# Batch 6 takes its gate logits with the gate weights as stationary operand, and the order's model gives the last batch's logits another duration

## The chip, the cores and the metric

The kernel runs on one core of one Trainium2 chip. The metric is the device time of one execution, in microseconds (us). The core's engines are named as in the profile: PE is TensorE's matmul, PEld its load of the stationary operand, DVE is VectorE, ACT is ScalarE, POOL is GpSimd, SP is SyncE.

## What is computed

Windowed attention (four heads with a plain window of 32 keys, four with a window of 32 keys that lie 4 apart) over 8 batches of 576 tokens gives 4608 rows of 512 values. Each row then goes to one of 8 experts, and the assignment is greedy over all pairs of token and expert:

```
x = attn(q, k, v)                     # (4608, 512), float32
logits = x @ w_gate                   # (4608, 8)
for idx in argsort(-logits.flatten()):        # best pair first
    tok, e = idx // 8, idx % 8
    if assigned[tok] < 0 and counts[e] < 576: # capacity of an expert
        assigned[tok] = e; counts[e] += 1
for e in range(8):
    out[assigned == e] = relu(x[assigned == e] @ w1[e]) @ w2[e]
```

## The kernel before, in words

There are two stages: `attention`, which also computes the logits, and `moe`, which searches the experts' thresholds (`R.alone` for the first), gathers the tokens, and runs two matmuls per expert. The first search needs the logits of all 4608 tokens, so the last logits of `attention` stand between the stages.

In `attention` the work is cut into 32 units, four for each batch b: unit u = 4b + 2 kind + ui, where kind 0 is the plain window and kind 1 the dilated one. On PE a unit runs a bfloat16 pass for the row maxima (L486), then three groups of scores (L503 for mask and maximum, L506 for the float32 product), then the product with the values in two groups (L514). ACT takes the exponential (L456), DVE divides by the sum (`weigh`, L520 and L526). For each batch, seven "turns" of three transposes each (L564) bring the rows into `xt` with the features on the partitions. A "keep" (L272 on ACT, L575 on DVE for the very last) copies each turn out of PSUM. The PSUM tiles of the values, the turns and the logits come from one pool of three (`PV`).

The logits have two forms.

- The weights stationary (`banks`, batches 0 to 5, L597 on): for each half of a batch, four matmuls, one per block of 128 features. The gate weights, padded to 32 columns, are the stationary operand and 288 tokens move. The four blocks land in four bands of 32 partitions. DVE copies the result to `L4` (L605), transposes on PE (`gates`, L616) turn it chunk by chunk of 128 tokens, and a DVE reduction (`settle`, L622) adds the four bands into `Lt`. All of `xt` of the batch must be there first.
- The tokens stationary (`tokens`, batches 6 and 7, L654): four steps, one per feature block. Each runs five matmuls (four chunks of 128 tokens and one of 64) with 8 columns moving. Steps 0 and 1 need the plain turns only, step 2 the turns of the first dilated unit, step 3 all of them. A copy on DVE (L664) and one on ACT (L272) bring the result into `Lt`. Each float32 matmul is recorded as two MATMULs, so a step shows as x10; a transpose is recorded as one.

A batch ends with `R.choose` (L869 to L879 on DVE: best expert and its key) and `coarse` (L755 on DVE, L760 on PE: counts against coarse thresholds). The counts of all chunks form one chain in order of the chunks. A batch of 576 tokens is 4.5 chunks, so an odd batch's first half chunk shares its column of `Lt` with the batch ahead. `DIRECT` is the first batch of the second form.

The order on each engine is written out by a planner (`Schedule.run`). Each step has a modelled cost, dependencies and a boost. `left` is the longest modelled path from a step to the end, with 180 added for each change of engine. `due` is the whole length minus `left` minus boost. A step with larger `left` plus boost is taken first. Where the first in line isn't ready, the planner fills in steps that end by the modelled start of the first plus a tolerance (800 on PE). The boost of unit u has -4680 u in it; values have 14500 more, the weights-stationary logits and batch 6's turns -5200, batch 7's turns and logits 3000.

Of the kernel before, what the change touches and what calls it, by code (L numbers as in the profile page):

```python
# [14 lines left out]
OP = mybir.AluOpType  # L15
AX = mybir.AxisListType
# [3 lines left out]
B, H, S, D = 8, 8, 576, 64  # L20
N = B * S
DM = H * D
NE, FF = 8, 1024
# [15 lines left out]
B_L, B_G, B_T, B_X, B_H, B_HL, B_Y, B_S, B_W = 23000, 27000, 15000, 0, 20000, 17000, 28000, -15000, 1500  # L39
RAW1, D_R, NQ, AHEAD_W = 8, 262, (2, 2), (3,)  # L40
ADDED, T_A, T_G = (("2", 0), ("1", 1), ("2", 1)), 4500, 4500
NS, B_E, DIRECT = (2, 2), 3000, 6
B_C = (0, 2500, 20000, 20000, 20000, 20000, 20000, 20000)
P_U, B_A, B_K, B_V, B_P, TOL_A, TOL_B, TOL_C, TOL_D = 4680, 15400, -5200, 14500, -105500, 650, 650, 300, 800
Q_ENG = (("POOL", "POOL", "POOL", "ACT"), ("DVE", "DVE", "ACT", "ACT"))
# [197 lines left out]
def attention(tc, ctx, C, load_const, T, xd, Lt, R):  # L243
    nc = tc.nc
# [5 lines left out]
    op = K.op  # L250

    def ring(pool, shape, dtype, name, n):
        return Ring([pool.tile(shape, dtype, name=f"{name}{i}") for i in range(n)])
# [13 lines left out]
    L4 = ring(pk, [128, 2 * S], F32, "L4", 1)  # L267
# [43 lines left out]
    ready = {}  # L311
# [69 lines left out]
    class Unit:  # L381
# [40 lines left out]
        def build(self):  # L422
# [56 lines left out]
            if ui == 1:  # L479
                for k, f in enumerate(stores(b, kind, xs)):  # L480
                    usex.append(op("SP", 475, f, Unit.xsd, -u * P_U - 5000, dma=128 * S * 4 * 2 / 4 / D_R))
            banks(self, xs, list(Unit.xsd), usex)

        def scan(self, c0, c1, pm):
# [58 lines left out]
    xt_ = {}  # L543

    def banks(un, xs, done, usex):

        b, kind, ui, u = un.b, un.kind, un.ui, un.u
        if ui == 0:
            if kind == 0:
                xt_[b] = []  # L550
            xt_[b, kind] = XT[kind].take()
        xt, oldt, uset = xt_[b, kind]
        for i in (() if kind == 0 and ui == 0 else range(3) if kind == 0 else (ui, 2 + ui)):
            pt = Buf(PV)

            def turn(i=i, pt=pt):
                t = pt.tile.rearrange("p (c x) -> p c x", c=4)
                for c in range(3):
                    if kind == 0:
                        src = xs[:, 3 * i + c].rearrange("p a d -> p (a d)")  # L560
                    else:
                        si, ch = divmod(i, 2)
                        src = xs[:, 3 * si + c, 2 * ch:2 * ch + 2].rearrange("p a d -> p (a d)")
                    nc.tensor.transpose(t[:, c], src, C["identf"])  # L564

            end = b == B - 1 and (kind, i) == (1, 3)

            def keep(i=i, pt=pt, act=nc.vector.tensor_copy if end else act):
                t = pt.tile[:, :384]
                if kind == 0:  # L570
                    act(xt[:, :, 192 * i:192 * i + 192].rearrange("p a (c i) -> p c a i", i=64),
                        t.rearrange("p (c a i) -> p c a i", c=3, a=2))
                else:
                    si, ch = divmod(i, 2)
                    act(xt[:, ch].rearrange("p (c i r) -> p r c i", c=3, r=DIL)[:, 2 * si:2 * si + 2],  # L575
                        t.rearrange("p (c a i) -> p a c i", c=3, a=2)[..., :48])

            late = B_K if b < B - 1 else B_E
            t = un.op("PE", 325, turn, done, late, pt)
            usex.append(t)  # L580
            k = un.op("DVE" if end else "ACT", 491 if kind == 0 else 620, keep, [t, *oldt], late)
            pt.users.append(k)
            xt_[b].append(k)
            if (kind, ui) == (1, 0):
                ch_.setdefault(b, []).append(k)
        if (kind, ui) != (1, 1):
            return
        if b >= DIRECT:
            return tokens(un)
        lg = L4_[b % 2] = []  # L590
        sm = []
        for j in range(2):
            pt = Buf(PV)

            def logits(j=j, pt=pt):
                for g in range(4):
                    nc.tensor.matmul(pt.tile[32 * g:32 * g + 32, :S // 2], wgp[:, g],  # L597
                                     xt_[b, g // 2][0][:, g % 2, 288 * j:288 * j + 288], start=True, stop=True)

            t = un.op("PE", 560, logits, [*xt_[b], ready["w"]], B_K, pt)  # L600
            for kk in range(2):
                xt_[b, kk][2].append(t)
            o = (b % 2) * S + 288 * j
            eng = "ACT" if b == B - 1 and j else "DVE"
            k = un.op(eng, 365, lambda o=o, pt=pt, eng=eng: (nc.vector.tensor_copy if eng == "DVE" else act)(  # L605
                L4.tiles[0][:, o:o + 288], pt.tile[:, :S // 2]), [t, *L4_["free"]], B_K)
            pt.users.append(k)
            lg.append(k)
            c0 = -(-b * S // 128) if j == 0 else sm[0][1]
            c0, c1 = (b * S // 128 if j == 0 else sm[0][1]), (b * S + 288 * (j + 1)) // 128  # L610
            pg = Buf(PV)

            def gates(c0=c0, c1=c1, pg=pg):
                for c in range(c0, c1):
                    o = (128 * c) % (2 * S)
                    nc.tensor.transpose(pg.tile[:, 128 * (c - c0):128 * (c - c0) + 128], L4.tiles[0][:, o:o + 128], C["identf"])  # L616

            t = un.op("PE", 107 * (c1 - c0), gates, [*L4_[0], *L4_[1]], B_K, pg)

            def settle(c0=c0, c1=c1, pg=pg):  # L620
                n = c1 - c0
                nc.vector.tensor_reduce(Lt[:, c0:c1], pg.tile[:, :128 * n].rearrange(  # L622
                    "p (c g e) -> p c e g", c=n, g=4)[:, :, :NE], axis=AX.X, op=OP.add)

            x = un.op("DVE", 60 + 35 * (c1 - c0), settle, [t], B_K)
            pg.users.append(x)
            sm.append((x, c1, t))
        L4_["free"] = [x[2] for x in sm] if b % 2 else []
        c0, c1 = b * S // 128, (b * S + S) // 128
        x = un.op("DVE", 800, lambda: R.choose(c0, c1), [x[0] for x in sm], B_K)  # L630
        coarse(c0, c1, x, B_P)

    def coarse(c0, c1, x, late):
        for c in range(c0, c1):
            g, used, use_ = PRE.take()
            f = op("DVE", 290, lambda c=c, g=g: R.coarse(c, g), [x, *used], late)
            counted[0] = op("PE", 60, lambda c=c, g=g: R.coarse_counts(c, g), [f, ready["c", 3], counted[0]], late)
            use_.append(counted[0])

    def tokens(un):  # L640

        b, u = un.b, un.u
        c0, c1 = b * S // 128, (b * S + S) // 128
        parts = [(c, 0, 128) for c in range(-(-b * S // 128), c1)]
        half = (c0, 64, 64) if b % 2 else (c1, 0, 64)
        late = B_K if b < B - 1 else B_E
        pt = Buf(PV)
        o = lambda c, p, n: pt.tile[p:p + n, NE * (c - c0):NE * (c - c0) + NE]

        def logits(gs):  # L650
            for c, p, n in parts + [half]:
                for g in gs:
                    t0 = 128 * c + p - b * S
                    nc.tensor.matmul(o(c, p, n), xt_[b, g // 2][0][:, g % 2, t0:t0 + n], wgp[:, g, :NE],  # L654
                                     start=(c == parts[0][0] and g == 0), stop=(g == 3), skip_group_check=True)

        t = un.op("PE", 550, lambda: logits([0]), [*xt_[b][:3], ready["w"]], late, pt)
        t = un.op("PE", 550, lambda: logits([1]), [t], late)
        t = un.op("PE", 550, lambda: logits([2]), [t, *ch_[b]], late)
        t = un.op("PE", 550, lambda: logits([3]), [t, *xt_[b]], late)  # L660
        for kk in range(2):
            xt_[b, kk][2].append(t)
        ca = parts[0][0]
        xs_ = [un.op("DVE", 200, lambda: nc.vector.tensor_copy(  # L664
            Lt[:, ca:c1], pt.tile[:, NE * (ca - c0):NE * (c1 - c0)].rearrange("p (c e) -> p c e", e=NE)), [t], late),
            un.op("ACT", 250, lambda: act(Lt[half[1]:half[1] + 64, half[0]], o(*half)), [t], late)]
        pt.users += xs_
        if b < B - 1:
            hl_.append(xs_[1])
        x = un.op("DVE", 1000, lambda: R.choose(c0, c1), [*xs_, *(hl_ if b == B - 1 else ())], late)  # L670
        coarse(c0, c1, x, B_P if b < B - 1 else late - u * P_U)

    ch_, hl_ = {}, []
# [40 lines left out]
    for u in range(4 * B):  # L714
        b = u // 4
# [754 lines left out]
```

## Time and profile before

| | |
|---|---|
| median of 3 runs | 720.18 us (719.60 to 720.63) |
| the profiled execution's own time | 720.37 us |
| its span, first to last instruction | 718.6 us |
| PE busy | 678.6 us, 94% of the span |
| DVE, ACT busy | 484.2 us, 291.1 us |
| granted TensorE clock, mean over the span | 0.961 of full speed |

The profile is of one execution, and times in it are counted from the span's start. "Granted clock" is the share of full speed that TensorE was given: 1.00 is 2.4 GHz and 0.50 is 1.2 GHz. `attention` takes about the first 211 us. Matmuls overlap in the pipeline, so in a list of them the step from one start to the next tells more than a duration.

### The profile page before, as it was taken

How to read it: one execution, taken by the hardware profiler on the slowest of the kernel's cores; microseconds unless marked ns; L12 is line 12 of the kernel's file. 1: busy time of each engine (PE TensorE's matmuls, PEld its weight loads, DVE VectorE, ACT ScalarE, POOL GpSimd, SP SyncE). 2: the span in 40 equal slices, each digit the busy share in tenths (PEclk: the TensorE clock that was granted, in tenths of full speed). 3: DMA queues.
4: the chain of work that ended last, by engine and by line, in shares of the span. 5: the costliest groups of instructions: out<-in, count | busy, mean ns of one | idle time of the engine just before them, and what ended most of it. 6: DMA issues, size and time to landing. Idle time of an engine off the chain costs nothing.

```text
span 718.6 us, 17416 instructions
## 1 busy us (share of the span) xinstructions
PE 678.6 (94%) x6598; PEld 596.5 (83%) x6598; DVE 484.2 (67%) x2081; ACT 291.1 (41%) x617; POOL 137.3 (19%) x204
## 2 busy tenths in 40 slices
PE   7899999999984799799999999999999999999995
PEld 5788889998973598589889879788978978988984
DVE  5578877698237689579679868868978963823300
ACT  3355454543310383575334423514533434423310
POOL 6111111100000332741410310311221031221011
PEclk9999999999975799999999999999999999999998
DMA  9999999972111674978223513511532383122001
GB/s 249 260 269 294 264 301 267 281 198 55 47 35 36 207 147 106 292 172 238 96 67 118 169 63 92 200 45 52 167 135 67 118 291 130 56 74 97 1 22 45
DMA packets 58525, 104.62 MB, mean 146 GB/s; under 512 B 6212, under 2 KB 27844, under 8 KB 58436
## 3 DMA queue, kind: packets, MB, share of 16 engines
q1 hardware_dynamic: 49096, 78.32, 38.0%
q0 software_dynamic: 9344, 25.17, 12.8%
q8 instruction: 52, 0.85, 0.5%
q14 instruction: 33, 0.27, 0.1%
HBM read 78.31 MB, written 18.87 MB: 135 GB/s over the span
## 4 chain that ended last, share of the span: by engine, by line
PE 74%; issue 11%; DVE 6%; DMA 4%; POOL 3%; ACT 1%; POOLq 0%; SPq 0%; DVEq 0%
PE ph L1290 24%; PE py L1332 15%; PE pS L506 9%; PE px L514 6%; PE px L564 3%; PE pS L503 3%; DMA xg<-xd,idx 2%; PE pm L486 2%; PE pz L768 2%; PE ptx L1253 2%; PE px L654 2%; PE py L1335 1%; PE py L1337 1%; POOL out L1358 1%; DMA qs<-in_qd 1%
## 5 line engine op out<-in xcount | busy, mean ns | idle before, releaser
L1332 PE MATMUL py<-w2h,hb 128*128 128x512 f32 x512 | 173.6, 403 | 1.4 <-ACT w2h L1127 1.3
L1290 PE MATMUL ph<-xh,w1h 128*128 128x256 f32 (+1 forms) x512 | 138.7, 301 | 0.0
L1290 PE MATMUL ph<-xl,w1h 128*128 128x256 f32 (+1 forms) x512 | 136.2, 297 | 0.0
L1290 PE MATMUL ph<-xh,w1l 128*128 128x256 f32 (+1 forms) x512 | 136.0, 296 | 0.0
L1332 PEld LDWEIGHTS py<-w2h,hb 128*128 128x128 f32 x512 | 97.3, 190 | 21.8 <-ACT w2h L1127 2.3
L1332 PE MATMUL py<-w2l,hb 128*128 128x512 f32 x256 | 101.3, 396 | 0.8 <-DVE w2l L1128 0.5
L1127 ACT ACTIVATE hb<-ph 128x256 fp32r<-128x256 f32 (+2 forms) x192 | 59.7, 346 | 103.1 <-PE ph L1290 102.3
L1290 PEld LDWEIGHTS ph<-xh,w1h 128*128 128x128 f32 x512 | 91.5, 190 | 0.4
L1290 PEld LDWEIGHTS ph<-xh,w1l 128*128 128x128 f32 x512 | 91.6, 190 | 0.0
L1290 PEld LDWEIGHTS ph<-xl,w1h 128*128 128x128 f32 x512 | 91.5, 190 | 0.0
L506 PE MATMUL pS<-q,k 128*80 128x96 f32 (+1 forms) x672 | 84.2, 267 | 0.0
L1358 POOL DMA_INDIRECT out<-y,idx x40 | 40.1, 1003 | 205.9 <-ACT y L1127 145.0
L456 ACT ACTIVATE E<-pS 96x384 f32<-96x384 f32 (+1 forms) x96 | 46.7, 486 | 71.5 <-PE pS L506 70.4
L1310 DVE SCALAR_TENSOR_TENSOR hb<-ph,hb 128x320 fp32r<-128x320 f32 (+1 forms) x128 | 57.4, 453 | 26.5 <-ACT hb L1127 22.5
L506 PEld LDWEIGHTS pS<-q,k 128*80 128x80 f32 (+1 forms) x672 | 69.7, 161 | 0.1
L1127 ACT ACTIVATE y<-py 128x512 f32<-128x512 f32 (+1 forms) x40 | 23.9, 596 | 104.9 <-PE py L1332 90.1
L493 DVE CUSTOM_DVE_ANT_0 junkm<-pm,const 128x80 bf16<-128x80 f32 (+1 forms) x336 | 59.4, 243 | 5.1 <-PE pm L486 4.5
L1332 PEld LDWEIGHTS py<-w2l,hb 128*128 128x128 f32 x256 | 48.8, 191 | 10.6 <-DVE w2l L1128 1.1
L514 PE MATMUL px<-v,E 81*64 81x65 f32 (+1 forms) x1344 | 47.7, 225 | 2.9 <-ACT E L456 2.4
L1127 ACT ACTIVATE w1h<-raw 128x512 fp32r<-128x512 f32 x64 | 38.5, 628 | 29.3 <-DVE oa L1060 22.0
L1239 POOL DMA_INDIRECT xg<-xd,idx x40 | 40.2, 1005 | 50.1 <-PE ph L1290 31.1
L1128 DVE TENSOR_TENSOR w2l<-raw,w2h 128x512 fp32r<-128x512 f32 x48 | 31.7, 685 | 26.4 <-ACT w2h L1127 22.9
(168 smaller groups left out, 1036.5 us busy)
## 6 DMA issues: line engine op xcount, KB each, us to landing
raw<-in_moe_w SPq DMA_DIRECT2D x128, 256.0 KB, 3.7
v<-in_vp SPq DMA_DIRECT2D x8, 780.0 KB
v<-in_vd SPq DMA_DIRECT2D x8, 650.0 KB
xd<-xs SPq DMA_DIRECT2D x16, 288.0 KB, 8.9
xd<-xs SPq DMA_DIRECT2D x32, 144.0 KB, 10.0
w2l<-raw POOLq DMA_DIRECT2D x16, 256.0 KB
qs<-in_qp SPq DMA_DIRECT2D x7, 576.0 KB, 8.6
k<-in_kp SPq DMA_DIRECT2D x7, 576.0 KB, 10.4
```

Of the source, the lines that this page charges most:

```text
L456: e = self.op("ACT", 380, lambda j=j, pS=pS: nc.scalar.activation(self.E[:self.nk, j * self.gs:j * self.gs + self.gs], pS.tile[:, :self.gs ...
L493: nc.vector.tensor_tensor_reduce(out=jk[:, c - c0, :nk], in0=pm[:, (c - c0) * nk:(c - c0 + 1) * nk], in1=mm[:, min(1, (c if self.kind == 0 ...
L503: nc.tensor.matmul(pS[:nk, c - c0], ls[:64 + n, c], self.r[:64 + n, :2 * nq], start=(c == c0), stop=False, skip_group_check=True)
L506: nc.tensor.matmul(pS[:nk, c - c0], self.Ks[c], self.Qm[c], start=False, stop=True, skip_group_check=True)
L514: nc.tensor.matmul(px[64 * a:64 * a + 64, c - c0], lh, self.V[c][a], start=True, stop=True)
L1127: act = lambda o, i, f=AF.Copy: nc.scalar.activation(o, i, f)
L1128: sub = lambda e, o, a, b: e.tensor_tensor(o, a, b, op=OP.subtract)
L1239: nc.gpsimd.indirect_dma_start(out=xg[:n], out_offset=None, in_=xd, in_offset=bass.IndirectOffsetOnAxis(ap=box[0][:n, m:m + 1], axis=0))
L1290: nc.tensor.matmul(o, a[:, d * 128:d * 128 + 128], b[:, d, c0:c1], start=((d, i) == pairs[0]), stop=((d, i) == pairs[-1]))
L1310: hl = op("DVE", 335 if j == 0 else 400, lambda: nc.vector.scalar_tensor_tensor(hb[:, CAP + c0:CAP + c1], o, 0.0, hb[:, c0:c1], op0=OP.max ...
L1332: nc.tensor.matmul(py, x, w, start=(f + i == 0), stop=(f == NF - 1 and i == 2))
L1358: s = nc.gpsimd.indirect_dma_start(out=out, out_offset=bass.IndirectOffsetOnAxis(ap=box[0][:n, m:m + 1], axis=0), in_=y[:n], in_offset=None)
```

## The change

`DIRECT` goes from 6 to 7: batch 6 takes its logits with the weights stationary, and only batch 7 with the tokens stationary. As batch 6 ends in half a chunk, its second half gets one transpose more (64 tokens, `over`) and one DVE reduction more, and batch 7's `choose` waits for that step in place of batch 6's copy on ACT. The modelled cost of each of batch 7's four steps goes from 550 to 1050. The extra transpose and reduction have no modelled cost.

```diff
-NS, B_E, DIRECT = (2, 2), 3000, 6
+NS, B_E, DIRECT = (2, 2), 3000, 7
...
-            def gates(c0=c0, c1=c1, pg=pg):
+            over = b == DIRECT - 1 and j == 1
+
+            def gates(c0=c0, c1=c1, pg=pg, over=over):
                 for c in range(c0, c1):
                     o = (128 * c) % (2 * S)
                     nc.tensor.transpose(pg.tile[:, 128 * (c - c0):128 * (c - c0) + 128], L4.tiles[0][:, o:o + 128], C["identf"])
+                if over:
+                    o = (128 * c1) % (2 * S)
+                    nc.tensor.transpose(pg.tile[:64, 128 * (c1 - c0):128 * (c1 - c0) + 128], L4.tiles[0][:, o:o + 64], C["identf"])
...
-            def settle(c0=c0, c1=c1, pg=pg):
+            def settle(c0=c0, c1=c1, pg=pg, over=over):
                 n = c1 - c0
+                if over:
+                    nc.vector.tensor_reduce(Lt[:64, c1], pg.tile[:64, 128 * n:128 * n + 128].rearrange(
+                        "p (g e) -> p e g", g=4)[:, :NE], axis=AX.X, op=OP.add)
...
+            if over:
+                hl_.append(x)
...
-        t = un.op("PE", 550, lambda: logits([0]), [*xt_[b][:3], ready["w"]], late, pt)
-        t = un.op("PE", 550, lambda: logits([1]), [t], late)
-        t = un.op("PE", 550, lambda: logits([2]), [t, *ch_[b]], late)
-        t = un.op("PE", 550, lambda: logits([3]), [t, *xt_[b]], late)
+        t = un.op("PE", 1050, lambda: logits([0]), [*xt_[b][:3], ready["w"]], late, pt)
+        t = un.op("PE", 1050, lambda: logits([1]), [t], late)
+        t = un.op("PE", 1050, lambda: logits([2]), [t, *ch_[b]], late)
+        t = un.op("PE", 1050, lambda: logits([3]), [t, *xt_[b]], late)
```

## Rows read from the trace of the kernel before

**Rows 1.** Stretches: us, then busy time (instructions) by engine, granted clock, DMA share, GB/s
```profile
170.00:180.00 10.00, 10.00 (x165) 9.52 (x162) 7.02 (x58) 4.80 (x10) 0.00 (x0) 1.00 0.21 51
180.00:185.00 5.00, 5.00 (x73) 4.68 (x72) 1.46 (x5) 1.21 (x4) 0.00 (x0) 1.00 0.11 25
185.00:190.00 5.00, 5.00 (x71) 4.70 (x70) 1.20 (x4) 1.85 (x4) 0.00 (x0) 1.00 0.06 15
190.00:195.00 5.00, 5.00 (x42) 4.96 (x42) 1.79 (x10) 2.02 (x5) 0.00 (x0) 0.70 0.47 107
195.00:200.00 5.00, 5.00 (x98) 4.91 (x97) 1.42 (x4) 1.46 (x3) 0.00 (x0) 0.96 0.01 3
...
210.00:215.00 5.00, 2.41 (x31) 1.70 (x31) 3.29 (x18) 0.17 (x1) 0.00 (x0) 0.50 0.00 0
```

**Rows 2.** Waits between 176 and 216 us: total us, times, longest
```profile
ACT E L456 <- PE pS L506: 9.5, 9, 3.1
...
PE pz L760 <- DVE pre L755: 1.7, 1, 1.7
```

**Rows 3.** PE in order of time, to batch 6's logits: start, us, line, shapes, count
```profile
170.76 1.18 PE L564 MATMUL px<-const,xs 128*128 128x128 f32 x9
...
181.65 1.27 PE L654 MATMUL px<-wgp,xt 128*128 128x8 f32 x10
182.85 0.37 PE L503 MATMUL pS<-R,const 73*96 73x128 bf16 x3
...
187.40 2.47 PE L654 MATMUL px<-wgp,xt 128*128 128x8 f32 x20
189.80 0.87 PE L564 MATMUL px<-const,xs 128*128 128x128 f32 x6
190.51 1.17 PE L654 MATMUL px<-wgp,xt 128*128 128x8 f32 x10
191.61 0.59 PE L564 MATMUL px<-const,xs 128*128 128x128 f32 x3
192.00 0.53 PE L503 MATMUL pS<-R,const 76*80 76x96 bf16 x4
```

**Rows 4.** Chain of waits around 165 us, batch 5's logits: start, us
```profile
163.50 0.62 PE px L597 x8
...
166.27 0.56 PE px L616 x5
```

**Rows 5.** DVE in order of time: the weights-stationary form's copies, and the last keep
```profile
164.94 0.82 DVE L605 COPY L<-px 128x288 f32<-128x288 f32 x2
...
206.70 0.66 DVE L575 COPY xt<-px 128x288 f32<-128x288 f32 x1 [2.78 <-PE px L564]
```

**Rows 6.** PE in order of time, scores of units 30 and 31
```profile
195.31 0.38 PE L503 MATMUL pS<-R,const 76*80 76x96 bf16 x4
...
198.04 0.36 PE L503 MATMUL pS<-R,const 76*80 76x96 bf16 x4
...
198.93 0.34 PE L503 MATMUL pS<-R,const 76*80 76x96 bf16 x4
```

**Rows 7.** Chain of waits, unit 31 and the tail of attention
```profile
199.95 0.66 PE px L564 x6
...
201.47 1.55 PE px L514 x48
203.02 2.40 PE px L654 x20
205.42 1.25 PE px L564 x6
206.67 3.95 PE px L654 x20
210.62 0.03 issue
```

**Rows 8.** A short stretch in the tail, columns as in rows 1
```profile
205.60:205.80 0.20, 0.20 (x3) 0.20 (x2) 0.00 (x0) 0.00 (x0) 0.00 (x0) 0.59 0.85 169
```

## Prediction

> **What bounds the kernel now.** I read the page first: PE is busy for 94% of the span, so PE is the engine to watch. Then I asked which stretch the edit touches: the end of attention, from the first unit of batch 7 (unit 28, at about 178 us) to the first search (about 212 us). I cut it into stretches [rows 1]. The reader is to see two things there. PE is busy for 5.00 of every 5 us up to 200, while DVE has between 1.20 and 1.79 us of work in 5 and ACT at most 2.02. And the granted clock is 1.00 up to 190, 0.70 between 190 and 195, and 0.50 after 210. The list of waits [rows 2] says the same of the engines: ACT waits for PE's scores (9.5 us in all), and PE's one wait of any size, 1.7 us, lies behind the last logits. So in this stretch a microsecond of PE work taken out is a microsecond off the end, as long as the order leaves no hole. Behind the last logits, choice, counts, search, gather and experts each hang on the step ahead (the expert weights' loads too, as the search names the expert), so all of it moves up together.
>
> **What goes.** Batch 6's four steps on L654, from start to start [rows 3]: step 0 from 181.65 to 182.85, 1.20 us; steps 1 and 2 from 187.40 to 189.80, 2.40; step 3 from 190.51 to 191.61, 1.10. Sum 4.70 us of PE. The two copies to `Lt` go too; they were on engines with room.
>
> **What comes.** Batch 5 shows the other form [rows 4]: two groups of four matmuls at 0.62 us (one of them stands), and five transposes at 0.56. Batch 6 needs as many: two of each chunk pair, 27 to 30, and one for the half chunk. That is 1.24 + 0.56 = 1.80; I take 1.85, because the five are split over two PSUM tiles. PE's balance is 1.85 - 4.70 = -2.85 us.
>
> On DVE come two copies, 0.82 us together [rows 5], and three small reductions, in place of one copy. That is about 1.3 us more in a stretch where DVE is idle for over 3 of every 5 us [rows 1], and I cost it at nothing. What hides it is PE's own queue: while DVE copies a half, unit 30's scores can run (0.89 us a group at full clock, from 198.04 to 198.93 [rows 6]). Were that cover gone, PE would stand for one copy and one reduction, up to 1 us. Batch 7's `choose` now waits for batch 6's last reduction. Behind it on DVE are only batch 7's own counts, and that reduction lies some 10 us earlier. No DMA is added or moved, and no step is moved past SP's or POOL's queue.
>
> **The clock in the middle.** Between 187.40 and 191.61 PE ran nothing but L654 and two turns [rows 3]. Right behind it the clock is low: unit 30's first two groups of scores, from 192.00 to 195.31, took 1.65 us each in place of 0.89 [rows 3, 6]. With the change that stretch holds matmuls that move 288 columns, with scores between them. Step 0 alone, at 181.65, had left the clock at 1.00 [rows 1]. I therefore expect no fall there. Its worth: from 191.61 to 195.31 are 3.70 us for one turn and two groups. At full clock two turns take 0.66 [rows 7], so one takes 0.33, and the groups 2 x 0.89: together 2.11. The gain is 1.6 us, and 0 if the clock falls anyway.
>
> **The model's new duration** changes what is taken first. Z is what the model has behind step 3, the same for all. Before, step 0 of batch 7 ranks at 4 x 550 + 3000 = 5200 + Z. A scores group of unit 31 ranks at 850 + 180 + 380 + 180 + 984 + 180 + 680 + 180 + 325 + 180 + 620 + 180 + 550 = 5469 + Z, so it goes first. After, step 0 is at 4200 + 3000 = 7200, step 1 at 6150, the scores at 5969, the turns of unit 31 at 2355 + 3000 = 5355, step 2 at 5100. So steps 0 and 1 go ahead of unit 31's scores. Step 2 fills the wait for unit 31's `weigh`: it would end at 1050 behind the values, and the turns can start at 180 + 680 + 180 = 1040, inside the tolerance. Then come the turns, and step 3 waits for the last keep.
>
> The tail now [rows 7]: values end at 203.02, steps 0 and 1 at 205.42, the turns at 206.67, steps 2 and 3 at 210.62. That is 7.60 us. After, for the same work at full clock: steps 0 and 1 elsewhere 2.40, step 2 1.20, the turns 0.66, the wait for the last keep 0.66 [rows 5] with about 0.1 of hand-over, 0.78, and step 3 1.20. Sum 6.24, a gain of 1.4. If the clock falls at the start of the turns, as it nearly does now (0.59 at 205.6 [rows 8]), they take 1.25 and step 3 half of 3.95, 1.98: sum 7.61, no gain. Below nothing it could go only by a further hole (a rival below). I take -0.6, nearer to no gain than to all of it, since the tail keeps L654 and transposes and gets a hole. What is late next is that keep.
>
> **Sum** against the profiled execution: 720.37 - 2.85 - 1.6 - 0.6 = 715.3. The profiled execution lies 0.2 above the median of the runs, so against that it would be 715.1; I keep 715.3, as a hand-over or two in the new order will cost something.
>
> **Rivals.**
>
> The clock falls in the middle all the same, either over the transposes that now come close together (units 27 and 29, and the five gates), or over batch 7's steps 0 and 1, which stand next to each other ahead of unit 31's scores. For it: in the tail the clock fell within 3 us of the start of such a pair [rows 7, 8]. Against it: scores stand on both sides now, and nine transposes at 170.76 left the clock at 1.00 [rows 1, 3]. Time: 715.3 + 1.6 = 716.9. The Trainium skill (TensorE: Matmul & The Clock Gate, Part 4: PE-mode transpose) says that full clock does not engage for the transpose mode, which does not count as busy in the same way; by it this rival would be the forecast, at 716.9, since the change puts five more transposes where L654 stood. The nine transposes just named speak against so strict a reading.
>
> The order of the tail stays, that is, the new duration does nothing. For it: step 1's margin over the scores is 181 of the model's units, and free PSUM tiles can decide too. Time: 715.3 + 0.6 = 715.9.
>
> A hole from the PSUM tiles. Batch 7's logits hold one of three tiles from step 0 on, and would hold it through unit 31's values, whose tiles come free with unit 30's keeps, two copies like the 0.66 of the last [rows 5]. Price two of them, 1.3 us; time 716.6. Against it: batch 6's logits held a tile in just this way from 181.65 on, and PE had no hole [rows 1].
>
> Not faster, or slower: the low clock, once there, stays through units 30 and 31. Its place is from steps 0 and 1 on. A group then takes 1.65 in place of 0.89, so each us of low clock loses 0.46. The change without its clock gain is worth 2.85 + 0.6 = 3.45, and the kernel now has 3.4 us of low clock here (3.0 at a mean of 0.70 in 190 to 195, 0.4 at 0.96 up to 200 [rows 1]). So nothing is gained at 3.4 + 3.45 / 0.46 = 10.9 us of low clock, and from there it is slower. Units 30 and 31 hold six groups, 2 x 1.55 of values and 0.66 of turns [rows 6, 7], 9.1 us at full clock; with all of it low they take 16.9: 715.3 + 7.8 = 723.1. Against it: now the clock came back at 195.31, behind two groups of scores [rows 6].
>
> **How the numbers follow.** Chances: the forecast 0.55; a fall in the middle 0.18; the tail's order unchanged 0.10; a hole from the tiles 0.05; a low clock that stays 0.12, of which 0.07 between 7.8 and 14 us of it and 0.05 beyond. A measurement of this kernel can tell about 0.2%, 1.4 us, from no change. So faster has 0.88, same 0.07, slower 0.05. The range: its low end is the whole tail gain (1.4 in place of 0.6, 714.5), the 0.2 to the median, and 0.7 for counts behind the logits that may still find the clock high: 713.6. Its high end is the balance of work alone, 720.37 - 2.85 = 717.5, and 0.7 for half of a hole: 718.2.
>
> **What would show it.** L654 at x40 (4 steps of 5 matmuls, two records each) and L597 at x112 (7 batches). In the stretches, PE full to unit 31's values and a clock of 1.00 from 180 to about 198. In order of time, batch 7's steps 0 and 1 ahead of unit 31's scores, one x10 of L654 ahead of the last turns, and one behind a hole of about 0.8 us. The last L654 ending near 205.6, and everything behind it as long as now. Wrong would be: a hole ahead of the gates (DVE not covered), a low clock between 190 and 200, or a stage behind the logits whose length changes by over 1 us.

## The result, and the profile after

| | before | after |
|---|---|---|
| median of 14 runs of each, measured side by side | 721.08 us | 718.17 us |
| ratio of the runs kept, with its 95% interval | | 0.9937 (0.9908 to 0.9967) |
| the profiled execution's own time | 720.37 us | 717.54 us |
| its span | 718.6 us | 715.8 us |
| PE busy | 678.6 us | 673.1 us |
| granted clock, mean over the span | 0.961 | 0.962 |

The ratio leaves out the slowest runs, four of the changed kernel and two of the kernel before, so it is not the ratio of the two medians, which is 0.9960. On the first median of before it means 715.6 us, against a forecast of 715.3. Two later comparisons of the same two kernels gave 0.9959 (0.9931 to 0.9988) and 0.9984 (0.9949 to 1.0018). So the kernel became faster by about 0.2 to 0.6%, and the last of the three intervals takes in no change at all. The mean of the three ratios is 0.9960, a gain of 2.9 us, where the forecast had 4.9: its sign is right, and its size lies just above the largest gain that was measured.

The stretches of the changed kernel, which answer to [rows 1] (us, then busy time and instructions by engine in the order PE, PEld, DVE, ACT, POOL, granted clock, DMA share, GB/s):

```profile
180.00:185.00 5.00, 5.00 (x82) 4.49 (x79) 3.57 (x39) 2.59 (x6) 0.00 (x0) 1.00 0.50 121
185.00:190.00 5.00, 5.00 (x75) 4.76 (x75) 1.79 (x7) 2.67 (x5) 0.00 (x0) 1.00 0.00 0
190.00:195.00 5.00, 5.00 (x86) 4.89 (x85) 0.47 (x3) 3.86 (x8) 0.00 (x0) 1.00 0.51 111
195.00:200.00 5.00, 5.00 (x73) 4.20 (x69) 3.62 (x16) 1.86 (x3) 0.00 (x0) 1.00 0.06 14
200.00:205.00 5.00, 5.00 (x86) 4.89 (x85) 1.39 (x6) 0.97 (x2) 0.00 (x0) 1.00 0.07 17
205.00:210.00 5.00, 3.68 (x38) 3.15 (x33) 1.41 (x3) 0.69 (x1) 0.00 (x0) 0.72 0.42 103
```

The clock is 1.00 all the way to 205 us, where it was 0.70 between 190 and 195. But PE now stands for 1.32 of the last 5 us. PE in order of time shows where, and it answers to [rows 3, 4, 6, 7] (start, us, line, shapes, count, then the idle time ahead and who ended it; the new lines L618 and L621 are the gates, L664 the narrow steps):

```profile
190.81 1.15 PE L564 MATMUL px<-const,xs 128*128 128x128 f32 x9
...
193.93 1.62 PE L514 MATMUL px<-v,E 81*64 81x65 f32 x48
195.48 1.18 PE L597 MATMUL px<-xt,wgp 128*32 128x288 f32 x16
196.59 0.55 PE L564 MATMUL px<-const,xs 128*128 128x128 f32 x3
196.97 0.38 PE L618 MATMUL px<-const,L 128*128 128x128 f32 x2
197.19 0.34 PE L503 MATMUL pS<-R,const 76*80 76x96 bf16 x4
...
198.05 0.38 PE L618 MATMUL px<-const,L 128*128 128x128 f32 x2
198.27 0.27 PE L621 MATMUL px<-const,L 128*64 128x128 f32 x1
198.38 0.49 PE L564 MATMUL px<-const,xs 128*128 128x128 f32 x3
198.71 1.17 PE L664 MATMUL px<-wgp,xt 128*128 128x8 f32 x10
199.81 0.36 PE L503 MATMUL pS<-R,const 76*80 76x96 bf16 x4
...
200.90 1.19 PE L664 MATMUL px<-wgp,xt 128*128 128x8 f32 x9
...
203.72 1.14 PE L664 MATMUL px<-wgp,xt 128*128 128x8 f32 x9
...
205.59 0.55 PE L564 MATMUL px<-const,xs 128*128 128x128 f32 x3
206.61 0.55 PE L564 MATMUL px<-const,xs 128*128 128x128 f32 x3 [0.47 <-DVE xs L526]
208.01 2.16 PE L664 MATMUL px<-wgp,xt 128*128 128x8 f32 x10 [0.85 <-DVE xt L575]
```

Batch 6's logits take 1.11 us (195.48 to 196.59), and its gates ran while scores filled the time of the copies. The reader is to see the two holes behind the last values, 0.47 us for the last division and 0.85 us for the last keep: steps 0, 1 and 2 all went ahead of the last values, and nothing is left to fill them. [rows 7] had no hole there. The last step then took 2.16 us in place of 1.20, as the clock was low again (0.72 on average between 205 and 210).

**One pair of profiles misleads here.** Between the spans lie 2.8 us, but at the end of the last L654 (L664 after) the two executions are only 0.4 us apart, 210.61 and 210.17. Both numbers are mixed with chance. The PE orders of the two kernels are the same up to about 55 us, and the same again behind the logits. Yet unit 7's third scores, the last piece of the common part, start at 54.39 before and at 58.07 after. One reason is a wait in the changed kernel, in a program part that both share (another is the scores behind it, which took 1.53 us in place of 0.85 at 55.18, at the low clock):

```profile
51.85 0.92 PE L514 MATMUL px<-v,E 81*64 81x65 f32 x24 [1.36 <-issue]
```

So I measure from unit 7's third scores to the end of the last L654, and call that **the stage**. It was 156.2 us before (54.39 to 210.61) and 152.1 after (58.07 to 210.17): 4.1 us less. Behind it lie 508.0 us before and 505.6 after, in one and the same program.

### The profile page after: what moved, and what is told of

The parts are those of the page before. It is cut to its first block, busy times and chain, and to the rows that moved or that the text cites. A ratio compares the mean times of both kernels' runs of the same rounds, so it can differ in the third digit from the quotient of the medians.

```text
span 715.8 us, 17384 instructions
## 1 busy us (share of the span) xinstructions
PE 673.1 (94%) x6577; PEld 590.1 (82%) x6579; DVE 485.2 (68%) x2085; ACT 292.0 (41%) x616; POOL 137.7 (19%) x204
## 4 chain that ended last, share of the span: by engine, by line
PE 73%; issue 12%; DVE 6%; DMA 4%; POOL 3%; ACT 1%; SPq 0%; POOLq 0%; DVEq 0%
PE ph L1300 24%; PE py L1342 15%; PE pS L506 9%; PE px L514 6%; PE pS L503 3%; PE px L564 3%; DMA xg<-xd,idx 2%; PE pm L486 2%; PE pz L778 2%; PE ptx L1263 2%; PE py L1345 1%; POOL out L1368 1%; PE py L1347 1%; DMA qs<-in_qd 1%; PE px L597 1%
## 5 line engine op out<-in xcount | busy, mean ns | idle before, releaser
L1342 PEld LDWEIGHTS py<-w2h,hb 128*128 128x128 f32 x512 | 96.7, 189 | 21.5 <-issue 2.4
L514 PEld LDWEIGHTS px<-v,E 81*64 81x64 f32 (+1 forms) x1344 | 43.1, 138 | 9.2 <-issue 2.9
```

The source lines that it names most:

```text
L514: nc.tensor.matmul(px[64 * a:64 * a + 64, c - c0], lh, self.V[c][a], start=True, stop=True)
L1342: nc.tensor.matmul(py, x, w, start=(f + i == 0), stop=(f == NF - 1 and i == 2))
```

## The experiments

Up to about 135 us PE waits here and there, for a load or for something that the profile does not name, and in some executions the clock is low near 60 us. I give the stage with and without these. For that part I count a us of low clock as 0.46 us lost, as in the forecast.

**The changed kernel and the kernel before once more.** No edit.

> The changed kernel once more, beside the kernel before on the same chip, for a second profile of each. My theory (2.85 us of PE work less, 1.6 us of low clock less in the middle, little in the tail): 3.5 to 5.5 us less than before; in the profile the clock is 1.00 from batch 6's logits to the last values, and from the last common PE instruction of the two orders (the row-maxima pass ahead of batch 0's first L597, about 55 us) to the end of the last L654 are 4 to 5 us less than before, as in the first profile. What lies ahead of that point and behind the last L654 runs the same program in both, so differences there (3.7 us more and 2.3 us less in the first pair of profiles) should not repeat. The rival, that the gain comes from behind the logits, expects those 2.3 us again.

> The kernel before, for a second profile of it. My theory: the clock falls again within 5 us of batch 6's steps 1 to 3, and unit 30's first scores then take 1.65 us a group. The time behind the last L654 differs from the first profile's 508.0 us by as much as that of two profiles of the changed kernel do, that is, by 1 to 2 us. If 508.0 repeats within 0.3 us, and the changed kernel's 505.6 too, the stage behind the logits has a part in the gain after all.

The stage was 151.9 us in the changed kernel (53.63 to 205.54, of it 0.5 us of waits at 56 and 103 us) and 157.5 in the kernel before (55.18 to 212.65, of it 1.3 us of waits at 59 and 82 us). The first profile of the changed kernel holds such a wait too, 0.5 us at 84 us. Without them the stage is 151.6 and 151.4 us in the changed kernel and 156.2 in both profiles of the kernel before: 4.7 us less. The runs of this comparison, at 0.9959, mean 3.0 us, less than the 3.5 to 5.5 that I had expected. Behind the logits were 507.5 us after and 504.7 before, so the first pair's 2.4 us were chance; they turned round, and the two profiles of before differ by 3.3 us there, more than I had expected. The clock fell in the second profile of before as in the first, behind batch 6's steps 1 to 3 (189.79 to 194.00 in this execution), and the scores behind them took 1.66 us a group:

```profile
190.00:194.00 4.00, 4.00 (x37) 3.87 (x36) 0.74 (x3) 0.87 (x2) 0.00 (x0) 1.00 0.43 93
194.00:199.00 5.00, 5.00 (x53) 4.98 (x53) 1.79 (x10) 1.77 (x5) 0.00 (x0) 0.66 0.18 47
...
195.71 0.53 PE L503 MATMUL pS<-R,const 76*80 76x96 bf16 x4
...
197.37 0.53 PE L503 MATMUL pS<-R,const 76*80 76x96 bf16 x4
```

**Each half of the change alone.**

The form alone is the changed kernel with the old durations, in all four steps:

```diff
-        t = un.op("PE", 1050, lambda: logits([0]), [*xt_[b][:3], ready["w"]], late, pt)
+        t = un.op("PE", 550, lambda: logits([0]), [*xt_[b][:3], ready["w"]], late, pt)
...
```

The duration alone is the kernel before with the new ones:

```diff
-        t = un.op("PE", 550, lambda: logits([0]), [*xt_[b][:3], ready["w"]], late, pt)
+        t = un.op("PE", 1050, lambda: logits([0]), [*xt_[b][:3], ready["w"]], late, pt)
...
```

> DIRECT = 7, but batch 7's steps keep the modelled cost of 550. My theory: the form of batch 6's logits carries the gain, so 2.85 + 1.6 = 4.4 us less than before (715.9 on the first profile's scale), within 1 us of the whole change; steps 0 and 1 of batch 7 stay behind unit 31's scores and the tail stays at about 7.6 us from the last values to the last L654. The rival (the new duration and the order that it makes carry the gain): within 1 us of the kernel before.

> DIRECT stays 6, but the steps have the modelled cost of 1050 (of batch 6 too, as the two share the line). My theory: PE's work is what it was, so only the tail and the clock can move; 0 to 1.5 us less than before. If the new order parts batch 6's steps with scores between, the clock may stay at 1.00 in the middle, and that would be worth up to 1.6 us more. The rival (the order carries the gain): 3 us or more less than before.

The form alone had a ratio to before of 0.9901 (0.9866 to 0.9935), the duration alone 0.9995 (0.9966 to 1.0023). The form carries the gain. The stage was 153.9 us with the form alone (56.17 to 210.10), of it waits of 1.7 us and 3.4 us of low clock near 60 us: some 150.6 without them, less than with the whole change. The tail was less at the low clock, too. The clock between 205 and 210 us was 0.56 on average in the kernel before and is 0.84 here; these are the two stretches:

```profile
205.00:210.00 5.00, 5.00 (x28) 4.91 (x28) 0.66 (x1) 0.68 (x1) 0.00 (x0) 0.56 0.37 88
...
205.00:210.00 5.00, 5.00 (x38) 4.87 (x38) 0.67 (x1) 0.68 (x1) 0.00 (x0) 0.84 0.34 86
```

With the duration alone it was 157.1 (52.77 to 209.87), of it a wait of 1.2 us at 103 us: 155.9 without it, only 0.3 less than before. That profile shows the wait and what became of the steps when the new duration drew them together behind unit 30's values:

```profile
103.01 0.25 PE L486 MATMUL pm<-k,q 128*128 128x80 bf16 x2 [1.20 <-issue]
...
195.54 1.27 PE L654 MATMUL px<-wgp,xt 128*128 128x8 f32 x10
196.74 0.87 PE L564 MATMUL px<-const,xs 128*128 128x128 f32 x6
197.45 2.38 PE L654 MATMUL px<-wgp,xt 128*128 128x8 f32 x20
...
190.00:199.00 9.00, 9.00 (x127) 8.70 (x127) 3.22 (x14) 4.49 (x9) 0.00 (x0) 1.00 0.25 58
199.00:203.50 4.50, 4.50 (x46) 4.46 (x46) 0.00 (x0) 0.53 (x2) 0.00 (x0) 0.62 0.00 0
```

Three steps (by their count batch 6's last and batch 7's first two) and two turns from 195.54 to 199.8, then the low clock: the same picture as batch 6's steps gave in the kernel before, a little later.

**The price of the clock by itself.** Two kernels add about the same PE time as idle work, at the same place of the changed order, behind batch 6's logits. One adds it as narrow steps, the other as matmuls that move 288 columns.

The narrow one:

```diff
                                      xt_[b, g // 2][0][:, g % 2, 288 * j:288 * j + 288], start=True, stop=True)
+                if b == DIRECT - 1 and j == 1:
+                    for g in range(4):
+                        for i in range(5):
+                            n = 128 if i < 4 else 64
+                            nc.tensor.matmul(pt.tile[:n, 320 + NE * i:320 + NE * i + NE],
+                                             xt_[b, g // 2][0][:, g % 2, 128 * i:128 * i + n], wgp[:, g, :NE],
+                                             start=True, stop=True)
```

The wide one:

```diff
+                if b == DIRECT - 1 and j == 1:
+                    for i in range(8):
+                        for g in range(4):
+                            nc.tensor.matmul(pt.tile[32 * g:32 * g + 32, :S // 2], wgp[:, g],
+                                             xt_[b, g // 2][0][:, g % 2, 288 * j:288 * j + 288], start=True, stop=True)
```

> The changed kernel, with batch 6's four tokens-stationary steps issued a second time behind its own logits, into PSUM columns that nobody reads (20 matmuls, idle work; the order of all else is unchanged). My theory, PE sets the end and such steps cost the clock: 4.7 us of work plus 1.6 us of scores at the low clock, so about 6 us more than the changed kernel, with a low clock for 3.4 us in the profile between 185 and 205. The rival, that PE's work is hidden here: within 2 us of the changed kernel.

> The changed kernel, with the second half's weights-stationary logits of batch 6 issued eight times more (32 matmuls that move 288 columns, idle work, the same order otherwise). That is 8 x 0.62 = 5.0 us of PE, as much as in the run with the narrow steps. My theory: about 5 us more than the changed kernel, and no low clock from 60 us to the last values; the difference to the narrow run, some 1.5 us, is the price of the clock alone. The rival, that the low clock comes from the wait or the phase and not from the narrow matmuls: the same time as the narrow run, and a low clock here as well.

PE in order of time and the clock, of the narrow kernel and then of the wide one (L603 and L602 are the added matmuls):

```profile
196.18 4.94 PE L603 MATMUL px<-wgp,xt 128*128 128x8 f32 x40
...
202.50 1.53 PE L506 MATMUL pS<-q,k 128*80 128x96 f32 x8
...
200.00:205.00 5.00, 5.00 (x37) 4.89 (x36) 1.08 (x5) 1.27 (x3) 0.00 (x0) 0.66 0.00 0
```

```profile
197.14 4.06 PE L602 MATMUL px<-xt,wgp 128*32 128x288 f32 x64
...
201.91 0.85 PE L506 MATMUL pS<-q,k 128*80 128x96 f32 x8
...
200.00:205.00 5.00, 5.00 (x63) 4.21 (x56) 2.42 (x13) 1.86 (x3) 0.00 (x0) 1.00 0.00 0
```

All four kernels of this order can be compared from the start of unit 29's values to the end of the last L664, which lies behind every chance event near 60 us. The changed kernel took 21.8 us (188.36 to 210.17) and 21.5 in its second profile (184.07 to 205.54; a third profile of it, below, took 25.2 us with a low clock of its own, so this comparison holds for executions in which the order itself has no fall ahead of the last values); the narrow one 27.7 (187.95 to 215.69), 6.1 more, as expected; the wide one 25.3 (189.02 to 214.27), 3.6 more, where 5.0 was expected. The wide matmuls ran faster than I had priced them, 4.00 us (197.14 to 201.14) in place of 5.0, so in these profiles the end moved by nearly all that was added: PE sets it. The narrow steps took 4.87 us, 0.9 more than the wide ones, and the end moved by 2.5 us more; the rest, 1.6 us, is the clock. The clock fell behind the narrow steps and not behind the wide ones. The runs bear out the order of the two only: ratios to before of 1.0097 (1.0056 to 1.0137) for narrow and 0.9968 (0.9930 to 1.0006) for wide, further apart than the stage can explain. Beside the changed kernel's 0.9937 to 0.9984 the wide ratio does not show the 3.6 us, and the narrow one shows more than 6.1. The wide execution took only 502.7 us behind the logits, against 505.6 and 507.5 in the changed kernel; why, and whether that holds for its other runs, stays open. That PE sets the end, and the price of the clock, rest on the profiles. The narrow execution also has a low clock of 3.4 us near 61 us.

**A step to fill the second hole.** Step 2 of batch 7 is held until the last two turns, which `tn_` lists.

```diff
-        t = un.op("PE", 1050, lambda: logits([2]), [t, *ch_[b]], late)
+        t = un.op("PE", 1050, lambda: logits([2]), [t, *ch_[b], *tn_[b]], late)
```

> The changed kernel, but step 2 of batch 7 also waits for the last two turns, so that it lies in the hole ahead of step 3. From the last values to the end of the last L654 the changed kernel has two holes, 0.47 and 0.85 us. My theory (the new duration takes away the cover of the last keep): the 0.85 us hole goes, and the time from unit 7's third scores to the last L654 falls by 0.6 to 0.9 us from 152.0; in the median up to 0.9 us less than the changed kernel, too little to be told apart by the runs alone. The rival, that holes cost nothing because the clock comes back in them: no less than 152.0.

```profile
206.81 0.80 PE L514 MATMUL px<-v,E 81*64 81x65 f32 x18 [0.26 <-ACT E L456]
...
208.56 0.55 PE L564 MATMUL px<-const,xs 128*128 128x128 f32 x3 [0.47 <-DVE xs L526]
208.94 2.37 PE L666 MATMUL px<-wgp,xt 128*128 128x8 f32 x20
```

The 0.85 us hole is gone, steps 2 and 3 run as one. The last values now wait 0.26 us for ACT's exponential: it is this wait that step 2 had filled in the changed kernel. From unit 29's values to the end it took 20.7 us (190.65 to 211.31) against 21.5 and 21.8: 0.8 to 1.1 less, where 0.6 to 0.9 was expected. The hole less the new wait is 0.6 us of that. The clock has a part too: in the changed kernel it was low from 207.2 and 204.1 us on, under the last step, and here it was 1.00 to the end of the last L666. The stage's raw number, 154.0 (57.33 to 211.31), holds a wait of 1.8 us and 3.4 us of low clock near 60 us, some 150.6 without them. The runs cannot tell so little: 0.9984 (0.9948 to 1.0019).

**The changed kernel and the form alone, side by side once more.** No further edit.

> The changed kernel beside the two others, on the same chip. Theory: 151.9 us from unit 7's third scores to the last L654 without waits and low clock near 60 us, the two holes of 0.47 and 0.85 us in the tail, clock at 1.00 from 180 us to the last values, and a ratio to before of 0.993 to 0.996.

> DIRECT = 7 with the old modelled cost of 550, once more beside the changed kernel. Theory (the new duration costs some 0.8 us, as it opens two holes in the tail): from unit 7's third scores to the last L654 150.5 to 151.5 us without waits and low clock near 60 us, no hole between the last values and the last L654, and a ratio to before 0 to 0.3% below that of the changed kernel. The rival (the new duration gains 0.6 us, as was forecast): 152.5 us or more, and a ratio above that of the changed kernel.

The form alone has the shorter stage again, and my number for the changed kernel did not hold. The two ratios do not tell the kernels apart, as their intervals overlap. The form alone: stage 150.9 us (53.92 to 204.77), ratio 0.9972 (0.9942 to 1.0002). Its steps stand behind the last values and cover both waits, step 0 that for the last division and steps 1 and 2 that for the last keep, so PE has no hole from the last turns on:

```profile
197.56 0.87 PE L564 MATMUL px<-const,xs 128*128 128x128 f32 x6
198.51 1.27 PE L664 MATMUL px<-wgp,xt 128*128 128x8 f32 x10
199.72 0.87 PE L564 MATMUL px<-const,xs 128*128 128x128 f32 x6
200.43 4.34 PE L664 MATMUL px<-wgp,xt 128*128 128x8 f32 x30
```

The changed kernel: stage 157.1 (53.87 to 210.99), of it 1.7 us of waits between 57 and 104 us, ratio 0.9984 (0.9949 to 1.0018). In this execution of it the clock fell at 199.2 us, at the end of batch 7's step 1, and did not come back before the search:

```profile
196.12 1.17 PE L664 MATMUL px<-wgp,xt 128*128 128x8 f32 x10
...
198.31 1.25 PE L664 MATMUL px<-wgp,xt 128*128 128x8 f32 x9
...
195.00:199.00 4.00, 4.00 (x51) 3.96 (x49) 1.94 (x12) 1.93 (x4) 0.00 (x0) 1.00 0.01 4
199.00:205.00 6.00, 6.00 (x62) 5.83 (x63) 0.75 (x2) 0.49 (x1) 0.00 (x0) 0.52 0.10 25
205.00:211.00 6.00, 5.03 (x36) 4.02 (x32) 1.41 (x3) 0.69 (x1) 0.00 (x0) 0.50 0.30 75
```

That is the rival of the low clock that stays: 11.8 us of it, and little is left of the gain, as the stage without its waits, 155.4 us, is only 0.8 less than the 156.2 of the kernel before. It was one of three profiles of this kernel; in the two kernels that share its order up to here, wide and step 2, it did not happen. The three profiles have a mean of 152.8 us without waits, 3.4 less than before, which is near the 2.9 us of the three ratios.

**Batch 7 as well in the weights-stationary form.**

```diff
-NS, B_E, DIRECT = (2, 2), 3000, 7
+NS, B_E, DIRECT = (2, 2), 3000, 8
...
+        late = B_K if b < B - 1 else B_E
...
-            over = b == DIRECT - 1 and j == 1
+            over = b == DIRECT - 1 and j == 1 and b % 2 == 0
...
-        coarse(c0, c1, x, B_P)
+        coarse(c0, c1, x, B_P if b < B - 1 else late - un.u * P_U)
```

`late` also stands in place of `B_K` in this form's steps.

> DIRECT = 8: batch 7 has the weights stationary as well. PE loses another 4.7 us of L654 and gets 1.85 us back. My theory: the tail from the last values is weigh 1.0, turns 0.7, keep 0.8, logits 1.3, copies 0.5, gates 0.6, reductions 0.4, some 5 us to the choice, against 7.1 + 0.45 in the run with the form alone and, with two steps of it moved ahead of the last values, 4.4 + 0.45 in the changed kernel. So 1 to 3 us less than the changed kernel, and the clock falls only in the holes of the tail. The rival (the chain through two copies and two transposes is longer than the steps it replaces): 0 to 2 us more.

> DIRECT = 8 once more, for a second profile. In the first, the coarse counts behind the logits started 154.8 us after unit 7's third scores, of which 1.8 us was a wait for a load near 60 us and about 1.6 us a low clock there: 151.4 without these, 2 us less than the changed kernel; but its six runs had a median 10.9 us below the kernel before. Theory A (the gain is the attention tail's, 2 to 3 us more than the whole change, and the rest was chance): ratio to before 0.988 to 0.993. Theory B (the clock is also held through part of the first search): the low clock behind the logits then lasts under 25 us in the profile in place of 27 to 34, and the ratio is 0.985 again.

This is faster than both kernels: 0.9850 (0.9806 to 0.9895) and 0.9909 (0.9878 to 0.9939). Theory A of the second run holds on its ratio. The low clock behind the logits lasts 27.3 us in the profile, not under 25, so theory B falls by its own sign. Its tail, in the second profile:

```profile
204.31 0.55 PE L564 MATMUL px<-const,xs 128*128 128x128 f32 x3 [0.15 <-DVE xs L526]
204.79 0.69 PE L598 MATMUL px<-xt,wgp 128*32 128x288 f32 x6
205.72 1.13 PE L598 MATMUL px<-xt,wgp 128*32 128x288 f32 x10 [0.25 <-DVE xt L575]
206.92 0.98 PE L619 MATMUL px<-const,L 128*128 128x128 f32 x5
209.41 0.99 PE L771 MATMUL pz<-oh,pre 128*128 128x8 bf16 x10 [1.51 <-DVE pre L766]
```

From unit 7's third scores to the coarse counts (L771 here, L760 before) it took 154.3 us (55.16 to 209.41), or 151.1 without a wait of 1.6 us and 3.4 us of low clock near 60 us; the first profile, 154.8 as it stands, gives 151.4 in the same way. The form alone took 152.5 (53.92 to 206.41) and the kernel before 157.9 (54.39 to 212.32). There is no narrow step of the logits left, no low clock between 64 us and the counts, and the holes in the tail are 0.26, 0.15 and 0.25 us. The stage accounts for 6.8 us of the 6.5 to 10.8 us that the two ratios mean; whether the rest of the first one has a cause stays open.

## Why the prediction was right, point by point

- **PE bounds the stage: shown in the profiles.** 4.0 us of wide matmuls moved the end by 3.6, and DVE's added work at 195 to 200 us (3.62 of 5) hid behind PE. The runs of the wide kernel do not bear it out by themselves.
- **The balance of work, -2.85 us: right, a little small.** L654 fell to x40 and L597 rose to x112. The logits took 1.11 us in place of 1.24, as both halves run back to back, and the gates (197.19 less 196.97, and 198.38 less 198.05) 0.55: 1.66 in place of 1.85.
- **The clock in the middle, -1.6 us: right in size, not certain.** Both profiles of before have the fall behind batch 6's steps, and the narrow kernel priced it at 1.6. It was gone in two profiles of the changed kernel. In the third a fall came at another place, behind batch 7's steps 0 and 1. The Trainium skill (TensorE: Matmul & The Clock Gate, Part 4: PE-mode transpose) says that full clock does not engage for the transpose mode. That is not what decides here: in the changed kernel nine transposes in a row, at 190.81, left the clock at 1.00, and the five of batch 6's gates did so too. By that rule the rival at 716.9 would have been the forecast.
- **The new duration, -0.6 us: wrong, and wrong in sign.** This is the step that failed: "So steps 0 and 1 go ahead of unit 31's scores. Step 2 fills the wait for unit 31's `weigh`", with "a gain of 1.4" down to "no gain" in the tail. Steps 0 and 1 did go ahead, of its last scores at least, but step 2 went ahead of the last values too (203.72), into their wait for the exponential. So nothing was left for the last division (0.47 us), and the last keep had the 0.85 us that I had counted. Form alone 150.6 and 150.9 us, whole change 151.6 and 151.4: in the profiles the duration costs 0.7 us where the clock holds, too little for the runs to show. And it puts steps 0 and 1 where a fall of the clock hits all of unit 31, at some 4 us in one profile of three (155.4 against 151.5). I had that fall among the rivals, at 0.18 and 0.12, as one of short and one of long duration; the long one came.
- **What made up for it, by luck.** The form alone gained more than I had summed: 156.2 less 150.8 is 5.4 us, against 2.85 + 1.6 = 4.45. In its two profiles only 1.7 and 1.9 us of the tail ran at the low clock, against 5.0 and 4.3 us before. At 0.46 us per us that is 1.3 us, which I had credited to the new duration alone and then mostly struck out. So the forecast's sum of 5.05 came near the 4.7 us of the two profiles in which the clock held, by two errors that nearly cancel. That the first ratio lay within 0.3 us of the forecast is luck as well: with the third profile's low clock, and over the three comparisons, the gain is 3.4 and 2.9 us.
- **Behind the logits nothing changed.** The three profiles of the changed kernel have 505.6, 507.5 and 508.4 us there, the two of before 508.0 and 504.7. The "over 1 us" that I had set as a sign of error was too tight: the same program varies by more. So was the "0.2%" that a measurement was to tell from no change: the intervals reach 0.3 to 0.35% to either side.

## What to carry to other kernels

Replace narrow matmuls (8 columns moving, a fresh 128-column operand for each) by wide ones where the result can be transposed afterwards: their own time was 4.7 us against 1.7 us here, and the clock that they can cost comes on top. A modelled duration nearer to the truth is no gain by itself: it moved three steps out of a tail in which they had covered two waits. And where runs vary by more than the effect, compare two traces from the last instruction that both orders share, without the waits wherever they lie, and more than one trace of each kernel.

## What the runs showed of the hardware

The clock fell to 1.2 GHz although PE was busy without a gap: between 185 and 190 us, ahead of the fall in the kernel before, it was busy for 5.00 of 5.00 us and its operand loads for 4.70 [rows 1]. In five profiles it fell between 190 and 205 us, ahead of the last values (the kernel before twice, the duration alone, the narrow kernel, the changed kernel's third), and ahead of each of these falls lay 2 to 5 us of narrow steps, with no more than turns, counts or a group of scores between them. 4.0 us of wide matmuls at the same place as the narrow ones had no such fall behind them. Narrow steps are not the only case: near 61 us the clock fell in five profiles without them, each time behind a wait of PE of 1.5 to 1.8 us (the form alone, narrow, step 2, and both of batch 7's form). The same order of steps 0 and 1 let the clock fall in one profile and not in two others, so what such an order costs is a matter of chances. Why it fell in that one is not settled by these runs.
